# Attention with soft mixture of experts on one core: whole columns of the last three w2 matrices, full output rows, and a tile of its own for the first pair's q and k

## The chip, the cores and the metric

The kernel runs on one core of a Trainium2 chip. The metric is device time in microseconds; the time before is 157.08 us, the median of 7 runs (156.41 to 157.62). TensorE, VectorE, ScalarE, GpSimd and SyncE are called PE, DVE, ACT, POOL and SP, as in the profile.

## The reference

There are two stages. The first is attention with 4 batches, 8 heads, 768 positions and a head dimension of 64; each head has either the full causal mask or a mask of sink positions and a window. Its output is laid out as x, 3072 tokens by 512. The second is a soft mixture of 8 experts with 4 slots each:

```python
logits = x @ phi                                   # 3072 x 32
d = softmax of logits over the tokens
slot_input = (d.T @ x).reshape(8, 4, 512)
for e in range(8):
    h = np.maximum(slot_input[e] @ w1[e], 0.0)     # w1[e]: 512 x 1024
    slot_out[e] = h @ w2[e]                        # w2[e]: 1024 x 512
c = softmax of logits over the slots
return c @ slot_out.reshape(32, 512)               # 3072 x 512, float32
```

All inputs and the output are float32 in memory.

## The kernel before

**Order of work.** The order of the instructions on each engine is the order in which the code is written; tiles give the waits. All loads go through POOL's DMA queue and are cast from float32 to bf16 on the way: q, k, v, phi, and w1 and w2 of the eight experts. A tile pool with two buffers (`raw`, used in `load_qk`, L106) holds the raw q and k, so the load of a third piece waits until the transposes of the first have read it. `load_qk([0])`, `load_qk([1])`, `load_v(0)` and the first w1 are issued before the loop; at the start of step 0 of the loop come `load_qk([2])` and `load_v(1)`.

**Attention.** The loop over `n` goes through 16 pairs of heads. A step computes the scores of pair `n` in six chunks (L167), their exponentials on ACT (L172), masks them on DVE (L184), multiplies the pair before with its values (L193) and transposes q and k of the pair after (L141). `w_load` spreads the loads of the weights over the loop; w1 is complete and w2 of experts 0 to 4 is issued there.

**The last three w2.** The w2 of experts 5, 6 and 7 have no place until attention lets go of memory: expert 5 takes the place of the masks, 6 and 7 those of the two exponential tiles. They are loaded in halves of 256 columns by `w_half` (L399): first the left halves of all three, then the right halves. The memory layout is `(fi fo) d -> fi fo d`, so that one partition reads 8 consecutive rows of w2; a half takes 256 columns of each of them.

**The experts.** After the slot inputs, the products with w1 (L481) and the transposes of the hidden layer (`turn`, L497), the products with w2 collect in two PSUM tiles, `sp[0]` for the left and `sp[1]` for the right 256 columns. They use 32 output partitions at a time, in four groups of partitions; `second` (L513) multiplies one expert. As expert 5, 6 and 7 have four rows only, their products may go to any of the four groups: what follows sums the groups. 24 small products (L530) give the sums by which an output row is divided (`rrow`).

**Output.** The output is 24 blocks of rows: partition `p` holds rows 24p to 24p+23. Each block is one product with `slot_out` (L541), scaled on DVE if its number is even (L545) and on ACT if odd (L543), and stored by a DMA together with its neighbours. The order before is this. The left columns of experts 5 to 7 are multiplied, `slot_out`'s left half is copied (L556), and the left halves of blocks 0 to 11 are made and stored from POOL's queue. Then come the right columns of experts 5 to 7, the copy of the right half (L560), blocks 12 to 23 in full, stored from SP's queue (L568), and at last the right halves of blocks 0 to 11, also from SP's queue (L554).

Of the kernel before, what the change touches and what calls it, by code (L numbers as in the profile page):

```python
# [10 lines left out]
F32 = mybir.dt.float32  # L11
BF16 = mybir.dt.bfloat16
I32 = mybir.dt.int32
ALU = mybir.AluOpType
ACT = mybir.ActivationFunctionType
# [23 lines left out]
def kernel(  # L39
# [13 lines left out]
    nc = tc.nc  # L53
    P = 128
    B, H, S, D = q.shape
    n_sink, window = int(n_sink), int(window)
    ES = moe_phi.shape[1]
    NE, DM, F = moe_w1.shape
    SPE = ES // NE
    scale = 1.0 / (D ** 0.5)  # L60
# [4 lines left out]
    raw = ent(tc.tile_pool(name="raw", bufs=2))  # L65
# [9 lines left out]
    def single(shape, dt, name, tag=None):  # L75
        return singles.tile(shape, dt, name=name, tag=tag or name)

    w1s = [single([P, 4, F], BF16, f"w1_{e}") for e in range(NE)]
    w2s = [single([P, 8, DM], BF16, f"w2_{e}") for e in range(NE - 3)] + [None] * 3
# [7 lines left out]
    rrow = single([P, 24], F32, "rrow")  # L87
# [7 lines left out]
    slot_out = single([P, DM], BF16, "slot_out")  # L95
# [9 lines left out]

    def load_qk(pairs, order="qk"):  # L106
        b, h, c = pairs[0] // 4, 2 * (pairs[0] % 4), 2 * len(pairs)
        t = raw.tile([P, 2, 2, S], BF16, tag="raw", name="raw")
        for which in order:
            src, d, z = (q, qraw, 0) if which == "q" else (k, kraw, 1)  # L110
            nc.gpsimd.dma_start(t[:, z, :len(pairs)],  # L111
                                src[b, h:h + c].rearrange("(y h) (p s) d -> (h p) y (s d)", h=2, s=12))
            for x, n in enumerate(pairs):
                d[n] = t[:, z, x]

    def load_v(m):
        b, h = m // 2, 4 * (m % 2)
        nc.gpsimd.dma_start(vbs[m % 3].rearrange("p h j d -> p (h j) d")[:, :, :D],  # L118
                            v[b, h:h + 4].rearrange("h (j p) d -> p (h j) d", p=P))
# [5 lines left out]
    w2v = [moe_w2[e].rearrange("(fi fo) d -> fi fo d", fo=8) for e in range(NE)]  # L125
    wi = [1]

    def w_load(upto):
        while wi[0] < min(upto, 2 * NE - 3):
            e = wi[0] % NE  # L130
            dst, src = ((w1s, w1v), (w2s, w2v))[wi[0] // NE]
            nc.gpsimd.dma_start(dst[e], src[e])
            wi[0] += 1
# [89 lines left out]
    def logits_exp(b):  # L223
        nc.scalar.activation(expT[:, b], lgs[b][:96], ACT.Exp, accum_out=colpart[:, b:b + 1])  # L224
# [29 lines left out]
                   allow_small_or_imprecise_dtypes=True)  # L254
    load_qk([1])
    load_v(0)
    nc.gpsimd.dma_start(w1s[0], w1v[0])

    V = nc.vector
# [3 lines left out]
    def keep_busy(t, count):  # L263
        for _ in range(count):
            nc.tensor.matmul(t, zero[:, :P], zero, start=True, stop=True)  # L265

    idle = pvp.tile([P, 512], F32, tag="pv", name="idle")
# [23 lines left out]
    def head_mask(h):  # L291
        V.tensor_scalar(msk[:, h], grade, thr[:, h:h + 1], None, op0=ALU.is_ge)
# [26 lines left out]

    for n in range(NP):  # L320
        if n == 0:
            load_qk([2])
            load_v(1)
        elif n == 1:
            load_qk([3])
        elif n == 2 or (n % 2 == 1 and n < 12):
            m = 2 if n == 2 else (n + 3) // 2
            load_qk([2 * m, 2 * m + 1])
            load_v(m)
        w_load(1 + 5 * (n + 1) // 8)  # L330
        if n == 0:
            nc.gpsimd.dma_start(phi, moe_phi.rearrange("(do di) s -> di do s", di=P))
        b, r = n // 4 - 1, n % 4
        last = n - 1

        scores(n, 0)
        if n >= 1:
            for i in range(3):
                pvmm(last, i)
        if b >= 0 and r == 2:  # L340
            logits_mm(b, (0, 1, 2, 3))

        scores(n, 1)
        if b >= 0 and r == 2:
            logits_exp(b)
        if n >= 1:
            norm(last, 0)
        if 0 < n < NP - 1:
            tq = transposes(n + 1, "q")
            evac(n + 1, "q", tq)  # L350
        mask(n, 0)
        if b >= 0 and r == 3:
            exp_tokens(b)

        scores(n, 2)
        if n >= 1:
            pvmm(last, 3)
        if n >= 2:
            x_transpose(n - 2)
        mask(n, 1)  # L360

        scores(n, 3)
        if 0 < n < NP - 1:
            tk = transposes(n + 1, "k")
        mask(n, 2)

        scores(n, 4)
        if 0 < n < NP - 1:
            evac(n + 1, "k", tk)
        if n >= 1:  # L370
            pvmm(last, 4)
        if n:
            vfar(n)

        scores(n, 5)
        if n == 0:
            vfar(0)
        if n >= 1:
            pvmm(last, 5)
            norm(last, 1)  # L380
        if b >= 0 and r == 3:
            dispatch_mm(b)
            slot_sum(b)
        if n == 0:
            evac(1, "q", transposes(1, "q"))
            evac(1, "k", transposes(1, "k"))
        if n < 3:
            far_mask(n + 1)
            for h in (2 * n + 2, 2 * n + 3):
                head_mask(h)  # L390
        elif n == 3:
            setup_late()


    w_load(2 * NE)
    left, right, full = slice(0, 256), slice(256, 512), slice(0, 512)

    def w_half(e, cs):
        nc.gpsimd.dma_start(w2s[e][:, :, cs], w2v[e][:, :, cs])  # L399

    w2s[5] = single([P, 8, DM], BF16, "w2_5", tag="msk")
    w_half(5, left)
    w2s[6] = ptp.tile([P, 8, DM], BF16, tag="pT", name="w2_6")
    w_half(6, left)


    def bank(t, shape=(P, 512), dt=F32):
        pool, tag = ((scp, "sc"), (trp, "tr"), (pvp, "pv"))[t]
        return pool.tile(list(shape), dt, tag=tag, name="bank")
# [27 lines left out]
    copies(1, 0)  # L437
    logits_mm(bl, (0, 1, 2))
    w2s[7] = ptp.tile([P, 8, DM], BF16, tag="pT", name="w2_7")
    w_half(7, left)  # L440
    for e in (5, 6, 7):
        w_half(e, right)
    x_transpose(last, 0, 3)
    x_transpose(last, 3, 6)
    copies(2, 0)
    idle = bank(2)
# [11 lines left out]
    idle = bank(2)  # L458
# [10 lines left out]
    cs = bank(1, (P, 1))  # L469
# [5 lines left out]
    for e4 in range(2):  # L475
        t = xp.tile([P, 2, 512], BF16, tag="xb", name="hs")
        for c in range(2):
            hp = bank(0 if e4 == 0 else 2)
            for do in range(4):
                for g in range(4):  # L480
                    nc.tensor.matmul(hp[32 * g:32 * g + 32], siT[:, do],  # L481
                                     w1s[4 * e4 + g][:, do, c * 512:(c + 1) * 512],
                                     start=(do == 0), stop=(do == 3))
# [6 lines left out]
    hT = {}  # L490
# [14 lines left out]
    sp = [t[:, 0, :256] for t in spt]  # L505
    idle = spt[1][:, 1]

    def second(e, xs=(0, 1), spread=False):
        e4, g = e // 4, e % 4
        for fo in range(8):  # L510
            c = fo % 4 if spread else g
            for x in xs:
                nc.tensor.matmul(sp[x][32 * c:32 * c + 32, :], hT[e4][:, fo, 32 * g:32 * g + 32],  # L513
                                 w2s[e][:, fo, 256 * x:256 * x + 256],
                                 start=(e4 == 0 and fo == 0), stop=(e == 7 and fo >= 4))

    turn(0)
    for fo in range(8):
# [2 lines left out]
                nc.tensor.matmul(sp[x][32 * g:32 * g + 32, :], hT[0][:, fo, 32 * g:32 * g + 32],  # L521
                                 w2s[g][:, fo, 256 * x:256 * x + 256], start=(fo == 0), stop=False)
    turn(1)
    second(4, spread=True)
    rp = bank(2, (P, 24))
    er = []
    for r in range(24):
        e = expR.rearrange("c (p r) -> c r p", r=24)[:, r]
        er.append(e)
        nc.tensor.matmul(rp[:, r:r + 1], e[:ES], ones[:ES], start=True, stop=True)  # L530
    V.reciprocal(rrow, rp)
    for e in (5, 6, 7):
        second(e, (0,), spread=True)


    NL = 12
    ov = out.rearrange("(p r) d -> p r d", r=24)

    def product(r, o, cs, t):
        op = bank(t, (P, cs.stop - cs.start))  # L540
        nc.tensor.matmul(op, er[r], slot_out[:, cs], start=True, stop=True)  # L541
        if r % 2:
            nc.scalar.activation(o, op, ACT.Copy, scale=rrow[:, r:r + 1])  # L543
        else:
            V.tensor_scalar(o, op, rrow[:, r:r + 1], None, op0=ALU.mult)  # L545

    def half_rows(cs, t0, groups, banks, eng):
        ots = [single([P, n, 256], F32, f"oh{t0 + x}", tag=f"w1_{t0 + x}") for x, n in enumerate((8, NL - 8))]
        r = 0
        for rows in groups:  # L550
            for _ in range(rows):
                product(r, ots[r // 8][:, r % 8], cs, banks[r % len(banks)])
                r += 1
            eng.dma_start(ov[:, r - rows:r, cs], ots[(r - 1) // 8][:, (r - rows) % 8:(r - 1) % 8 + 1])  # L554

    V.tensor_copy(slot_out[:, left], sp[0])  # L556
    half_rows(left, 0, (2, 2, 4, 4), (1, 2), nc.gpsimd)
    for e in (5, 6, 7):
        second(e, (1,), spread=True)
    V.tensor_copy(slot_out[:, right], sp[1])  # L560
    r = NL
    for t, groups in enumerate(((1, 1, 2), (4,), (4,))):
        ot, base = single([P, 4, DM], F32, f"ot{t}", tag=f"w1_{4 + t}"), r
        for rows in groups:
            for _ in range(rows):
                product(r, ot[:, r - base], full, (1, 2)[r % 2])
                r += 1
            nc.sync.dma_start(ov[:, r - rows:r, :], ot[:, r - rows - base:r - base])  # L568
    half_rows(right, 2, (4, 4, 4), (1, 2), nc.sync)


# [33 lines left out]
```

The softmax here doesn't subtract the row's maximum and nothing guards it: scores larger than these inputs give would overflow.

## Time and profile before

| What | Value |
|---|---|
| Median of 7 runs | 157.08 us |
| Profiled execution, its own time | 157.49 us |
| Span of the profiled execution | 155.7 us |
| PE, DVE, ACT, POOL busy | 119.8, 107.2, 110.4, 41.2 us |
| Mean granted TensorE clock | 0.891 |
| HBM read, written | 52.49 MB, 6.29 MB |
| Loads of a whole w1 or w2 (13, 1024 KB in bf16) | median 17.5 us from issue to landing |
| Loads of half a w2 (6, 512 KB in bf16) | median 16.3 us from issue to landing |

The span is from the first to the last instruction; the time of an execution is 1.8 us longer than the span of the profiled one. The time to landing of a DMA includes its wait in the queue behind the DMAs issued before it. The row that tells of the DMA engines gives the mean busy share of the 16 of them; a share over 1 in a narrow window means that packets of one engine overlap.

### The profile page before, as it was taken

The page shows a single profiled execution, that of the slowest core. Times are in us where ns is not written, and L with a number is a line of the kernel's source. Part 1 is how long each engine was busy: PE and PEld are TensorE (multiplying, and loading weights), DVE is VectorE, ACT ScalarE, POOL GpSimd, SP SyncE. Part 2 cuts the span into 40 slices and gives each one's busy share as a digit, 9 for nine tenths or more (in the row PEclk, how much of TensorE's full clock was granted, in tenths as well). Part 3 has the DMA queues.
Part 4 walks back from the last instruction along what each step waited for, and adds up shares of the span by engine and source line. Part 5 has one row for each costly group of instructions (what it writes and reads, how often), then busy time and mean ns, then how long its engine had stood idle before and what let it go on. Part 6 is the DMA issues. An engine that isn't in the chain of part 4 may idle for free. (4 is left out here: it accounts for less than half of the span.)

```text
span 155.7 us, 5049 instructions
## 1 busy us (share of the span) xinstructions
PE 119.8 (77%) x2237; PEld 75.7 (49%) x2239; DVE 107.2 (69%) x247; ACT 110.4 (71%) x148; POOL 41.2 (26%) x57
## 2 busy tenths in 40 slices
PE   6766597888597979979779989797887988949500
PEld 2324365555355656556456556564552476514300
DVE  2896279999958769879688897786854331719700
ACT  3286479989789898999998999999643311608700
POOL 7673033720350080070048200000453000510000
PEclk9965559999959999999999999999999999557965
DMA  3999999999999999999999999999999999997995
GB/s 44 163 170 203 177 211 207 198 183 184 222 213 201 191 211 200 187 221 193 188 223 192 188 226 208 213 223 208 225 210 192 198 198 197 184 344 288 415 355 183
DMA packets 40535, 32.85 MB, mean 211 GB/s; under 512 B 26050, under 2 KB 37826, under 8 KB 38594
## 3 DMA queue, kind: packets, MB, share of 16 engines
q0 software_dynamic: 38208, 27.82, 115.6%
q1 hardware_dynamic: 2306, 4.72, 8.1%
q8 instruction: 17, 0.28, 0.6%
q14 instruction: 4, 0.03, 0.1%
HBM read 52.49 MB, written 6.29 MB: 378 GB/s over the span
## 5 line engine op out<-in xcount | busy, mean ns | idle before, releaser
L172 ACT ACTIVATE pT<-sc 128x1024 bf16<-128x1024 f32 (+1 forms) x96 | 83.8, 922 | 10.6 <-PE sc L167 9.8
L167 PE MATMUL sc<-Tq,Tk 64*128 64x256 bf16 (+3 forms) x320 | 37.2, 297 | 13.6 <-ACT Tk L151 10.2
L193 PEld LDWEIGHTS <-pT 128*128 128x128 bf16 x672 | 25.2, 100 | 12.5 <-issue 8.3
L184 DVE TENSOR_TENSOR pT<-pT,msk 128x1024 bf16<-128x1024 bf16 (+1 forms) x48 | 29.4, 639 | 0.2 <-ACT pT L172 0.2
L193 PE MATMUL pv<-vb,pT 128*128 128x65 bf16 x352 | 27.9, 198 | 0.3 <-DVE xb L202 0.3
L193 PE MATMUL pv<-vf,pT 128*128 128x65 bf16 x320 | 25.5, 198 | 0.0
L167 PEld LDWEIGHTS <-Tk 64*128 64x128 bf16 x320 | 11.3, 95 | 22.9 <-ACT Tk L151 13.2
L141 PEld LDWEIGHTS <-raw 64*64 64x64 bf16 x768 | 16.1, 115 | 11.0 <-issue 8.5
L111 POOL DMA_DIRECT2D raw<-in_q_dram x10 | 6.4, 641 | 50.9 <-PE tpk L141 49.7
L148 DVE COPY Tq<-tpq 128x768 bf16<-128x768 bf16 x16 | 15.3, 956 | 6.1 <-PE tpq L141 5.9
L202 DVE TENSOR_TENSOR xb<-pv,rs 128x384 bf16<-128x384 f32 x32 | 17.8, 557 | 1.1
L151 ACT COPY Tk<-tpk 128x768 bf16<-128x768 bf16 x16 | 12.8, 803 | 4.8 <-PE tpk L141 4.8
L201 DVE RECIPROCAL rs<-pv 128x6 f32<-128x6 f32 x32 | 6.2, 194 | 12.5 <-PE pv L193 12.3
L118 POOL DMA_DIRECT2D vb<-in_v_dram x8 | 11.6, 1452 | 1.1 <-issue 0.9
L399 POOL DMA_DIRECT2D w<-in_moe_w_dram x6 | 5.3, 882 | 24.4 <-PE sc L167 22.2
L141 PE MATMUL tpk<-ident,raw 64*64 64x64 bf16 x384 | 9.6, 200 | 2.3 <-DVE Tq L148 2.3
L141 PE MATMUL tpq<-ident,raw 64*64 64x64 bf16 x384 | 9.9, 203 | 1.7 <-DMA raw<-in_q_dram 1.7
L541 PE MATMUL bank<-slot_out,expR 128*128 128x256 bf16 (+1 forms) x35 | 9.4, 385 | 1.9 <-DVE slot_out L556 0.5
L210 PE MATMUL tpx<-ident,xb 128*128 128x128 bf16 x96 | 8.1, 218 | 2.0 <-ACT expT L224 1.1
L211 DVE COPY xT<-tpx 128x768 bf16<-128x768 bf16 (+1 forms) x17 | 9.0, 529 | 0.8 <-PE tpx L210 0.8
L543 ACT ACTIVATE oh<-bank,rrow 128x256 f32<-128x256 f32 x12 | 5.3, 474 | 4.3 <-PE bank L541 4.1
L541 PEld LDWEIGHTS <-expR 128*128 128x128 bf16 x36 | 5.3, 153 | 6.1 <-issue 5.2
(86 smaller groups left out, 116.4 us busy)
## 6 DMA issues: line engine op xcount, KB each, us to landing
w<-in_moe_w_dram POOLq DMA_DIRECT2D x13, 1024.0 KB, 17.5
vb<-in_v_dram POOLq DMA_DIRECT2D x8, 384.0 KB, 12.0
w<-in_moe_w_dram POOLq DMA_DIRECT2D x6, 512.0 KB, 16.3
raw<-in_q_dram POOLq DMA_DIRECT2D x6, 384.0 KB, 9.0
raw<-in_k_dram POOLq DMA_DIRECT2D x6, 384.0 KB, 10.2
out_dram<-ot SPq DMA_DIRECT2D x2, 1024.0 KB, 4.6
out_dram<-oh SPq DMA_DIRECT2D x3, 512.0 KB, 6.3
out_dram<-oh POOLq DMA_DIRECT2D x2, 512.0 KB, 5.4
```

Source lines behind the costliest of these rows:

```text
L118: nc.gpsimd.dma_start(vbs[m % 3].rearrange("p h j d -> p (h j) d")[:, :, :D], v[b, h:h + 4].rearrange("h (j p) d -> p (h j) d", p=P))
L141: nc.tensor.transpose(tp[po, s, :], src[po, 64 * s:64 * s + 64], ident[po, po])
L148: nc.vector.tensor_copy(o, i)
L151: nc.scalar.copy(o, i)
L167: nc.tensor.matmul(sc[:, hh, at:at + 128 * cnt], kT[n][po:po + 64, j * 128:(j + 1) * 128], qT[n][po:po + 64, i0 * 128:(i0 + cnt) * 128], s ...
L172: nc.scalar.activation(pT[n][:, :, o:o + ln], sc[:, :, :ln], ACT.Exp, scale=scale)
L184: nc.vector.tensor_mul(x, x, m)
L193: nc.tensor.matmul(pv[n][:, i % 3, hh, :], pT[n][:, hh, o:o + 128], vv[:, hh, j, :D + 1], start=(j == 0), stop=(j == i))
L202: nc.vector.tensor_mul(xb[b][:, 3 * half:3 * half + 3, h * D:(h + 2) * D].rearrange("p i (h d) -> p i h d", h=2), pv[n][:, :, :, :64], rs. ...
L210: nc.tensor.transpose(tp[:, i * 128:(i + 1) * 128], xb[b][:, i, hp * 128:(hp + 1) * 128], ident)
L211: nc.vector.tensor_copy(xT[:, hp, i0 * 128:i1 * 128], tp[:, i0 * 128:i1 * 128])
L541: nc.tensor.matmul(op, er[r], slot_out[:, cs], start=True, stop=True)
```

## The change

Three things are changed.

1. The first pair's q and k get a tile of their own (`raw0`), so that the two buffers of `raw` serve from pair 1 on. `load_qk([2])` moves from the start of the loop, where it stood behind the load of the first w1, to a place ahead of that load.
2. The w2 of experts 5 and 6 are loaded whole, in one DMA each; that of expert 7 in two pieces, of which the first holds six of the eight `fo` (768 KB in bf16) and the second the last two (256 KB), both with all columns.
3. The products with w2 are done for both halves of the columns at once, expert by expert, with two warming products (`keep_busy`) ahead of expert 7. Behind the second piece of expert 7 stand four products, one in each group of partitions. Then `slot_out` is copied, the left half on DVE and the right half on ACT, and 24 full output blocks are made; blocks 0 and 1 are made in halves, of which DVE scales the left and ACT the right. All stores go through SP's queue, in groups of 1, 1, 2 and five times 4 blocks. The early left halves are gone.

```diff
     def load_qk(pairs, order="qk"):
-        t = raw.tile([P, 2, 2, S], BF16, tag="raw", name="raw")
+        if pairs == [0]:
+            t = single([P, 2, 1, S], BF16, "raw0")
+        else:
+            t = raw.tile([P, 2, 2, S], BF16, tag="raw", name="raw")
...
     load_v(0)
+    load_qk([2])
     nc.gpsimd.dma_start(w1s[0], w1v[0])
...
         if n == 0:
-            load_qk([2])
             load_v(1)
...
-    w_half(5, left)
+    nc.gpsimd.dma_start(w2s[5], w2v[5])
-    w_half(6, left)
+    nc.gpsimd.dma_start(w2s[6], w2v[6])
...
-    w_half(7, left)
-    for e in (5, 6, 7):
-        w_half(e, right)
+    for fos in (slice(0, 6), slice(6, 8)):
+        nc.gpsimd.dma_start(w2s[7][:, fos], w2v[7][:, fos])
...
-    second(4, spread=True)
+    second(4, range(8), (0, 0, 1, 1, 2, 2, 3, 3))
+    second(5, range(8), (0, 0, 1, 1, 2, 2, 3, 3))
...
     V.reciprocal(rrow, rp)
-    for e in (5, 6, 7):
-        second(e, (0,), spread=True)
+    second(6, range(8), (0, 0, 1, 1, 2, 2, 3, 3))
+    keep_busy(idle, 2)
+    second(7, range(6), (0, 0, 1, 1, 2, 2, 3, 3))
+    second(7, range(6, 8), (0, 1, 2, 3))
...
-    V.tensor_copy(slot_out[:, left], sp[0])
-    half_rows(left, 0, (2, 2, 4, 4), (1, 2), nc.gpsimd)
-    for e in (5, 6, 7):
-        second(e, (1,), spread=True)
-    V.tensor_copy(slot_out[:, right], sp[1])
+    V.tensor_copy(slot_out[:, :256], sp[0])
+    nc.scalar.copy(slot_out[:, 256:], sp[1])
...
-    for t, groups in enumerate(((1, 1, 2), (4,), (4,))):
+    for t, groups in enumerate(((1, 1, 2), (4,), (4,), (4,), (4,), (4,))):
+        ot, base = single([P, 4, DM], F32, f"ot{t}", tag=f"w1_{t}"), r
...
+                if r < 2:
+                    for x in range(2):
+                        cs = slice(256 * x, 256 * x + 256)
+                        op = bank((1, 2)[x], (P, 256))
+                        nc.tensor.matmul(op, er[r], slot_out[:, cs], start=True, stop=True)
+                        if x:
+                            nc.scalar.activation(o[:, cs], op, ACT.Copy, scale=scale)
+                        else:
+                            V.tensor_scalar(o[:, cs], op, scale, None, op0=ALU.mult)
+                else:
+                    op = bank((1, 2, 0)[r % 3])
+                    nc.tensor.matmul(op, er[r], slot_out, start=True, stop=True)
...
             nc.sync.dma_start(ov[:, r - rows:r, :], ot[:, r - rows - base:r - base])
-    half_rows(right, 2, (4, 4, 4), (1, 2), nc.sync)
```

More of the change, by code (lines that the diff above doesn't have):

```diff
@@ L395 @@
     w_load(2 * NE)
-    left, right, full = slice(0, 256), slice(256, 512), slice(0, 512)
-    def w_half(e, cs):
-        nc.gpsimd.dma_start(w2s[e][:, :, cs], w2v[e][:, :, cs])
     w2s[5] = single([P, 8, DM], BF16, "w2_5", tag="msk")
-    w_half(5, left)
+    nc.gpsimd.dma_start(w2s[5], w2v[5])
     w2s[6] = ptp.tile([P, 8, DM], BF16, tag="pT", name="w2_6")
-    w_half(6, left)
+    nc.gpsimd.dma_start(w2s[6], w2v[6])
     def bank(t, shape=(P, 512), dt=F32):
@@ L506, with second @@
     idle = spt[1][:, 1]
-    def second(e, xs=(0, 1), spread=False):
+    ends = {(0, 0): 6, (1, 1): 6, (0, 2): 7, (1, 3): 7, (1, 0): 4, (0, 1): 5, (1, 2): 2, (0, 3): 3}
+    def second(e, fos, groups):
         e4, g = e // 4, e % 4
[L510 to L515, printed above, removed]
+        for z, (fo, x) in enumerate((fo, x) for fo in fos for x in range(2)):
+            c = groups[z % len(groups)]
+            nc.tensor.matmul(sp[x][32 * c:32 * c + 32, :], hT[e4][:, fo, 32 * g:32 * g + 32],
+                             w2s[e][:, fo, 256 * x:256 * x + 256], start=False,
+                             stop=(e == 7 and ends[x, c] == fo))
     turn(0)
@@ L531 @@
     V.reciprocal(rrow, rp)
-    for e in (5, 6, 7):
-        second(e, (0,), spread=True)
-    NL = 12
-    ov = out.rearrange("(p r) d -> p r d", r=24)
[L539 to L549, printed above, removed]
+    second(6, range(8), (0, 0, 1, 1, 2, 2, 3, 3))
@@ L550, in half_rows @@
+    keep_busy(idle, 2)
[3 more added lines that the diff above has]
+    nc.scalar.copy(slot_out[:, 256:], sp[1])
+    ov = out.rearrange("(p r) d -> p r d", r=24)
+    r = 0
+    for t, groups in enumerate(((1, 1, 2), (4,), (4,), (4,), (4,), (4,))):
+        ot, base = single([P, 4, DM], F32, f"ot{t}", tag=f"w1_{t}"), r
         for rows in groups:
             for _ in range(rows):
-                product(r, ots[r // 8][:, r % 8], cs, banks[r % len(banks)])
@@ L553, in half_rows @@
-                r += 1
-            eng.dma_start(ov[:, r - rows:r, cs], ots[(r - 1) // 8][:, (r - rows) % 8:(r - 1) % 8 + 1])
-    V.tensor_copy(slot_out[:, left], sp[0])
-    half_rows(left, 0, (2, 2, 4, 4), (1, 2), nc.gpsimd)
-    for e in (5, 6, 7):
-        second(e, (1,), spread=True)
-    V.tensor_copy(slot_out[:, right], sp[1])
-    r = NL
-    for t, groups in enumerate(((1, 1, 2), (4,), (4,))):
[L563 to L566, printed above, removed]
+                o = ot[:, r - base]
@@ new lines @@
+                scale = rrow[:, r:r + 1]
+                if r < 2:
[10 more added lines that the diff above has]
+                    nc.tensor.matmul(op, er[r], slot_out, start=True, stop=True)
+                    if r % 2:
+                        nc.scalar.activation(o, op, ACT.Copy, scale=scale)
+                    else:
+                        V.tensor_scalar(o, op, scale, None, op0=ALU.mult)
```

## The prediction

> **What bounds the kernel now.** I read the DMA rows by windows first, then the chain that ended last, then the tail of the timeline engine by engine, then single DMAs from issue to landing. The windows (columns: stretch, its length, TensorE clock, DMA share, GB/s):
>
> ```profile
> 12.00:16.00 4.00, 0.50 1.01 207
> ...
> 92.00:96.00 4.00, 1.00 1.07 223
> ...
> 128.00:132.00 4.00, 0.99 1.45 197
> 132.00:136.00 4.00, 0.50 1.23 187
> 136.00:140.00 4.00, 0.50 1.01 334
> 140.00:144.00 4.00, 0.73 0.74 286
> 144.00:148.00 4.00, 1.00 1.02 416
> 148.00:152.00 4.00, 0.62 1.01 354
> ```
>
> From 4 us on the 16 DMA engines are full in every window until 140 us. Loads run near 200 GB/s (as written, in bf16; twice that is read), stores near 400. The one hole is in 140 to 144 (share 0.74): the stores' first data are not ready yet. The chain of waits (start, length, what) says the same:
>
> ```profile
> 116.64 0.47 PE bank L265 x2
> 117.11 20.95 DMA w<-in_moe_w_dram
> 138.05 0.04 issue
> 138.09 0.64 PE bank L513 x7
> 138.76 0.44 DVE slot_out L560
> ...
> 139.24 1.01 PE bank L541 x2
> ```
>
> The last right half of w2 (issued at 117.11, landed at L = 138.05) ends the loads; all compute is waiting for it. Behind it come a short chain and the stores. The kernel is thus a stream of loads, a gap, and a stream of stores, and what counts is how much of the stores lies behind L. The stores:
>
> ```profile
> 134.06 3.03 POOL L554 DMA_DIRECT2D out_dram<-oh  x4 [16.07 <-DVE oh L545]
> 140.64 4.22 SPq L568 DMA_DIRECT2D out_dram<-ot  x5
> 145.41 2.05 SPq L554 DMA_DIRECT2D out_dram<-oh  x2
> ```
>
> The four early stores (12 left half rows, 1.57 MB) are issued at 134.06 to 136.3 and take 4.7 to 5.7 us to land, so until 142.0. They fill the DMA engines while the last loads and the chain behind L are under way (334 GB/s in 136 to 140). The other 4.72 MB are issued from 140.64 on.
>
> **The change, part by part. Early load of pair 2: 0 on the time.** It removes this wait of PE (and 1.2 us of POOL's for the buffer):
>
> ```profile
> 18.35 0.85 PE L141 MATMUL tpq<-ident,raw 64*64 64x64 bf16 x24 [1.67 <-DMA raw<-in_q_dram]
> ```
>
> Both DMAs of pair 2 pass one DMA on POOL's queue, w1 of expert 0 (1024 KB), which lands about 2 us later and is first read at 121 us. `load_v(1)` and phi stay behind both. Compute may run up to 1.7 us earlier, or nothing if pair 3, which is loaded no earlier, stops it again. It doesn't matter: the DMA queue has work throughout and its sum is unchanged, and PE then waits for w2 at the end in any case. Its bounds are 0 and, if compute set the end, -1.7; a loss needs the queue to run dry, and it holds 4 us or more of work. I take 0.
>
> **Whole w2 instead of halves: L moves from 138.05 to 136.6.** Asked one at a time, the last whole loads (L132) were issued at 83.4, 83.9, 84.4, 85.8 and 87.8 and took 18.2, 22.5, 26.9, 30.3 and 33.2 us: they landed at 101.6, 106.4, 111.3, 116.1 and 121.0, 4.85 us apart. The six halves landed at 123.7, 127.2, 129.5, 132.2, 135.4 and 138.05. That is 17.0 us for 3 MB, with steps of 2.3 to 3.5. The regular step is about 2.65 (15.9 in all); 1.1 us are irregular. Both long steps have an instruction fetch on the DMA engines just before them; the queue table gives 17 of these with a 0.6% share, 0.6% x 16 x 155.7 / 17 = 0.9 us of one engine each, and a load has landed only when the slowest engine is done. Three whole loads are 3 x 4.85 = 14.55; the last piece of 256 KB is in packets of 2 KB, between the 512 B of the halves (5.3 us per MB) and the 8 KB of whole loads (4.85), so at most 0.1 more. That gives L = 121.0 + 14.65 = 135.65 without the irregular part, and 136.75 with all of it. PE's program up to there has the same length within some ten instructions, so the fetches come at about the same places: I take 136.6.
>
> Here a rule stands against the change. The Trainium skill, "DMA: Bandwidth & Descriptors", section Specifications, puts the smallest transfer for the full rate at 512 B. A half row of w2 in bf16 is just 512 B, and by the rule whole rows gain nothing: L would be 138.0 and the sum 1.4 us worse. The rows (2.65 us against 4.85 / 2 = 2.43 for 512 KB) decide for a gain of 0.2 us per half; a part of it could be the irregularity, which is why the upper end of my range keeps it out.
>
> **No early stores: does L gain by that too?** The first is issued at 134.06, behind all loads in the same queue, so an engine can turn to it only when its own share of the loads is done. I take 0; the bound on the other side is the rival below.
>
> **The chain behind L: -0.7.** Before, from L to the first store's issue: 140.64 - 138.05 = 2.6 us, made of eight products in two rounds on the four groups (0.64), the copy (0.42 and waits), a product of 512 columns (0.62 until DVE starts) and its scaling (0.74). After: one round of four (-0.2), both copies side by side (DVE 0.42; ACT's nearest row, 128x256 scaled in L543, 0.47: +0.05), a product of 256 columns (-0.2) and two scalings of 256 side by side (0.47 instead of 0.74: -0.3). 2.6 - 0.65 = 1.9 us.
>
> **PE's work ahead of L: 0.** The products of expert 5 move ahead of the 24 small ones, with 16 more products (0.5 us from 16 in 0.82). They and expert 6 end near 132.4 and two warming products follow; expert 7's first piece lands near 135. The wait of some 3 us covers them.
>
> **The stores: +3.5 us.** Before, from the first issue at 140.64, eight full rows (2.1 MB) are landed at 147.2 (issue 143.3 + 3.9), 6.6 us later; the next four at 144.5 + 5.3 = 149.8, so 2.6 us per MB; the three half groups 1.5 us each for 0.5 MB, until 154.35; the end of the span follows 1.35 later. Sum 6.6 + 2.6 + 4.5 + 1.35 = 15.05, and 155.7 - 140.64 = 15.06. After: eight rows 6.6, four groups of four rows 4 x 2.63 = 10.5, and 1.35: 18.5 us. So +3.45: the half rows' 1.57 MB behind L get cheaper by 0.6, and 1.57 MB more at 2.63 per MB come behind L, 3.95. DVE and ACT don't bound this: 4 rows take them 2 x 0.74 = 1.5 us, a store of them 2.63. Nor does PE: at half clock a 512-column product takes 0.43, four take 1.7. SP's issue of a full-row store is 0.33 to 0.42.
>
> **Sum.** 136.6 + 1.9 + 18.5 = 157.0 of span against 155.7: +1.3. The profiled execution's own time is 157.49, 0.4 above the median of 157.08, which its neighbours also reach (156.41 to 157.62), so I put the difference on the median: 158.4.
>
> **The rivals.**
>
> - The irregular part of the loads disappears (the fetches fall on an engine that is ahead) and the first rows follow faster than before. L = 135.65, span 156.05 or a little less: 157.4, the same. For it: whole loads before 121 land 4.85 apart although fetches go on there as well.
> - The kernel gets faster, because the early stores had held back the last loads. Place: the window 132 to 136, where the rate falls to 187 GB/s as stores start. At 197 GB/s the halves would have ended by 135.4 on average instead of 138.05; with 1.25 for whole rows L = 134.1, span 134.1 + 20.4 = 154.5, time 155.9. It decides as soon as L is below 135.3, where the span equals 155.7. Against it: the step before the last half (132.2 to 135.4) was as long with no store under way.
> - The stores don't keep 400 GB/s for so long: the same page's limit per core for HBM is 358 GB/s. Then 6.29 MB take 17.6 instead of 16.5 (2.63 per MB): about 159.5, or 160 if the first megabyte also starts late. The rows, two groups at 2.6 us, speak against it, and 354 GB/s in 148 to 152, with half rows in it, for it.
>
> **How the numbers follow.** A measurement of this kernel can tell about 0.5% from no change (156.3 to 157.9). Likeliest, 0.57: exposed stores with most of the irregular part, 158.4 (own range 157.8 to 158.9). Same, 0.25: 157.4 (156.9 to 157.9). Faster by held-back loads, 0.08: 155.9. Slow stores, 0.10: 159.5 and more. Slower: 0.54 of the first and the last case, 0.64. Same: 0.03 + 0.23 + 0.01 = 0.27. Faster: 0.09. The range leaves out most of the last two cases: 156.9 to 159.3.
>
> **What would show it.** Right: the last w2 piece lands at 135.7 to 136.8; the first store is issued 1.9 us later; DMA share drops well under 0.7 for some 3 us behind L and before it as engines finish one by one; from then on full-row groups land 2.6 us apart, the last 17 us after the first issue; PE's 1.67 us wait at 18 us is gone and L132's landings are not moved by more than 0.3 us. Wrong: L132's last landing moved (the early load did something to the stream), L under 135.3, or groups landing under 2.45 us apart.

## The result, and the profile after

The changed kernel takes 158.42 us (median of 27 runs, 157.56 to 160.44) against 157.25 us for the kernel before (64 runs): a ratio of 1.0092, 95% interval 1.0073 to 1.0111. It is some 1.4 us slower; the ratio leaves out, for both kernels, the executions more than 1.5% above the fastest, and so is a little larger than that of the medians. The forecast was 158.4 us, and a span of 157.0 us; the profiled execution has a span of 157.1 us and a time of its own of 158.89 us.

The windows of the changed kernel, in the same columns as before (stretch, length, TensorE clock, DMA share, GB/s):

```profile
124.00:128.00 4.00, 1.00 1.01 210
128.00:132.00 4.00, 1.00 1.03 212
132.00:136.00 4.00, 0.60 0.44 85
136.00:140.00 4.00, 0.50 0.10 37
140.00:144.00 4.00, 0.62 0.89 357
144.00:148.00 4.00, 1.00 1.04 426
148.00:152.00 4.00, 0.73 1.02 424
152.00:156.00 4.00, 0.50 0.80 330
```

Two things have changed. Loads of whole rows move 210 to 212 GB/s until 132 us, where the halves moved 197. And from 132 to 140 us the DMA engines run empty: their busy share is 0.44 and then 0.10, where it was over 1 before. The trace shows when each of the 16 engines reports its share of the last load: the first at 132.31, the last at 136.65, on average at 134.1. So the average engine stands idle for 2.5 us ahead of the last landing, and only the rest of the hole is the chain behind it. The early stores had filled both.

Between 132 and 144 us the kernel before moved (187 + 334 + 286) x 4 us = 3.23 MB and the changed one (85 + 37 + 357) x 4 us = 1.92 MB. The missing 1.31 MB take 3.3 us at 400 GB/s; that is what the early stores had been worth. Some 2 us of it come back, by an estimate from the windows. Up to 132 us the changed kernel has moved 26.21 MB and the one before 25.88, which is 0.8 us. Behind 144 us it has more left to move (4.72 MB against 3.74), but without half rows it moves that at some 400 GB/s against 361, which is 1 us for 3.74 MB.

The chain of waits that ended last (start, length, what):

```profile
112.96 0.52 POOL w L439
113.48 23.17 DMA w<-in_moe_w_dram
136.65 0.04 issue
136.69 0.45 PE bank L511 x4
137.15 0.42 DVE slot_out L537
137.57 0.04 issue
137.61 1.01 PE bank L551 x4
138.62 4.28 PE bank L558 x10
```

The last piece of w2 lands at L = 136.65 us instead of 138.05. Four products, the copies and the products of the first blocks follow; the first store is issued at 138.73:

```profile
138.73 9.34 SPq L564 DMA_DIRECT2D out_dram<-ot  x8
```

Before, 15.1 us passed from the first store behind the last load to the end of the span; now it is 157.1 - 138.73 = 18.4 us. Counted from L, it was 17.7 us to the end and is now 20.5. So the last load lands 1.4 us earlier, what follows takes 2.8 us longer, and the difference is the 1.4 us of the result.

### The profile page after: what moved, and what is told of

Its sections match the earlier page's. It is cut to its first block, busy times and chain, and to the rows that moved or that the text cites. A ratio compares the mean times of both kernels' runs of the same rounds, so it can differ in the third digit from the quotient of the medians.

```text
span 157.1 us, 5010 instructions
## 1 busy us (share of the span) xinstructions
PE 119.3 (76%) x2229; PEld 75.0 (48%) x2231; DVE 106.5 (68%) x241; ACT 109.6 (70%) x144; POOL 34.8 (22%) x51
## 5 line engine op out<-in xcount | busy, mean ns | idle before, releaser
L170 PE MATMUL sc<-Tq,Tk 64*128 64x256 bf16 (+3 forms) x320 | 36.7, 294 | 14.1 <-ACT Tk L154 10.5
L196 PE MATMUL pv<-vb,pT 128*128 128x65 bf16 x352 | 27.4, 196 | 0.3 <-DVE xb L205 0.3
L558 PE MATMUL bank<-slot_out,expR 128*128 128x512 bf16 x22 | 8.0, 500 | 0.6 <-ACT ot L560 0.6
L562 DVE TENSOR_SCALAR ot<-bank,rrow 128x512 f32<-128x512 f32 x11 | 8.0, 749 | 0.6 <-PE bank L558 0.2
L560 ACT ACTIVATE ot<-bank,rrow 128x512 f32<-128x512 f32 x11 | 7.3, 688 | 1.3 <-PE bank L558 1.0
L213 PEld LDWEIGHTS <-xb 128*128 128x128 bf16 x96 | 6.3, 100 | 2.8 <-issue 2.7
```

Of the source, the lines that this page charges most:

```text
L170: nc.tensor.matmul(sc[:, hh, at:at + 128 * cnt], kT[n][po:po + 64, j * 128:(j + 1) * 128], qT[n][po:po + 64, i0 * 128:(i0 + cnt) * 128], s ...
L196: nc.tensor.matmul(pv[n][:, i % 3, hh, :], pT[n][:, hh, o:o + 128], vv[:, hh, j, :D + 1], start=(j == 0), stop=(j == i))
L213: nc.tensor.transpose(tp[:, i * 128:(i + 1) * 128], xb[b][:, i, hp * 128:(hp + 1) * 128], ident)
L558: nc.tensor.matmul(op, er[r], slot_out, start=True, stop=True)
L560: nc.scalar.activation(o, op, ACT.Copy, scale=scale)
```

## The experiments

Times scatter by some 0.6 us from one execution to the next (standard deviation), so what a profile shows is also given as the time from L to the end of its span. That leaves out when the loads happened to end.

**The first part alone, and all but the first part.** The first kernel adds the early load to the kernel before; the second takes it out of the changed kernel.

```diff
-        t = raw.tile([P, 2, 2, S], BF16, tag="raw", name="raw")
+        if pairs == [0]:
+            t = single([P, 2, 1, S], BF16, "raw0")
+        else:
+            t = raw.tile([P, 2, 2, S], BF16, tag="raw", name="raw")
...
     load_v(0)
+    load_qk([2])
...
-            load_qk([2])
             load_v(1)
```

> The kernel before with the first part of the change alone: raw0 for the first pair and the load of pair 2 ahead of the first w1. My theory: 0 (within 0.3 us of before); PE's wait of 1.67 us at 18 us is gone, and the last w2 half still lands at 138.0, give or take 0.5. Rival: the early load shifts the stream of loads (in the profile of the changed kernel the last whole load ahead of experts 5 to 7 landed at 122.0 instead of 121.0); then the last half lands near 139.0 here and the time is 1 us worse than before.

> The changed kernel without the first part: pair 0 in the shared buffers, the load of pair 2 back behind the first w1. My theory: the same as the changed kernel, 158.4 (within 0.3). Rival, by which the early load delays the loads by 1.0 us: 157.4, with the last piece of w2 landing near 135.7.

Measured: alone on the kernel before 1.0024 (0.9989 to 1.0059), 157.62 against 157.34 us, last half landed at 137.7. The changed kernel without it: 159.28 us, 1.0110 (1.0074 to 1.0145), not told apart from the changed kernel's 1.0092, with the last piece at 137.2. Taking the early load out did not bring the landing back to 135.7, so it is not what moved it. In the changed kernel PE's wait at 18 us is gone, as the transposes of pair 2 show (timeline: start, length, instruction). But a wait of the same kind stands at a later pair, where the kernel before has none:

```profile
16.70 0.85 PE L144 MATMUL tpq<-ident,raw 64*64 64x64 bf16 x24
...
30.50 0.85 PE L144 MATMUL tpq<-ident,raw 64*64 64x64 bf16 x24 [1.09 <-DMA raw<-in_q_dram]
```

In the kernel with the early load alone this wait is 2.67 us. So the early load moves the wait to a later pair, much as the prediction had held possible. The end of attention has no common direction either: the last exponential ends at 113.3 us with the early load alone and at 111.4 before, at 109.9 in the changed kernel and at 110.4 without the early load. Of all this no gain reaches the end.

**Half loads in the changed kernel.** Everything else stays, so this parts the rows' length from the early stores.

```diff
...
-    nc.gpsimd.dma_start(w2s[5], w2v[5])
+    w_half(5, left)
...
-    nc.gpsimd.dma_start(w2s[6], w2v[6])
+    w_half(6, left)
...
-    for fos in (slice(0, 6), slice(6, 8)):
-        nc.gpsimd.dma_start(w2s[7][:, fos], w2v[7][:, fos])
+    w_half(7, left)
+    for e in (5, 6, 7):
+        w_half(e, right)
```

> The changed kernel with the w2 of experts 5 to 7 loaded as before, in six halves of 256 columns, left ones first; no early stores. My theory (short rows make the loads slower, the early stores did not hold them back): the last half lands at 138.0, give or take 0.5, as before; behind it come the 16 products of expert 7 instead of four, so the first store is issued some 3.0 us later and the time is 2.0 to 2.6 us above the changed kernel, about 160.7. Rival of the rule of 512 B (row length doesn't matter): the last half lands at 136.6, the time is 0.6 to 1.0 above the changed kernel. Rival of the held-back loads: without early stores the halves are all landed by 135.4, and the time is near that of the changed kernel or below it.

Measured: 160.69 us, 1.0201 (1.0151 to 1.0250). From its chain of waits:

```profile
117.41 20.44 DMA w<-in_moe_w_dram
137.85 0.04 issue
137.90 1.31 PE bank L517 x12
139.20 0.42 DVE slot_out L543
```

L is 137.85 with no early store under way, so the early stores had not held the loads back. From there to the end it takes 21.1 us, against 17.7 in the kernel before, whose L is nearly the same. So leaving the early stores out costs 3.4 us by the profiles, of which 0.6 lie in the first eight blocks, whose chain is longer here; by the times it is 2.0% or 3.2 us. Loading whole instead of in halves, with the shorter chain that goes with it, gives back 1.7 us (1.0201 against 1.0092). The two together are the change's 1.4.

The last whole load landed at 121.54 here, and the six halves took 16.3 us; in the changed kernel the same 3 MB took 14.65. Taken on the engine that finishes first, which leaves out what delays single engines, the 3 MB take 15.92 to 15.93 us in all three kernels that load them in halves (here and with the early load alone as well as before, with and without early stores). They take 15.48 with expert 5 whole, 15.04 with experts 5 and 6 whole, and 14.64 to 14.65 in the five profiles of kernels that load as the changed one does: 0.4 us for each expert. The rule of 512 B that the prediction cites, by which the rows' length would not matter, does not hold here: rows of 512 B cost 1.3 us per 3 MB more than the longer ones (8 KB, and 6 and 2 KB for expert 7). The number of packets changes with the rows, and the runs do not part the two. The first store is issued at 140.79, 2.9 us after L.

**The long chain in the changed kernel.**

```diff
-    nc.scalar.copy(slot_out[:, 256:], sp[1])
+    V.tensor_copy(slot_out[:, 256:], sp[1])
...
-                if r < 2:
+                if r < 0:
```

> The changed kernel with the longer chain behind the last piece: both halves of slot_out copied on DVE, blocks 0 and 1 made as full products. My theory: 0.4 for the second copy, 0.2 for the product of 512 columns and 0.3 for its scaling on one engine, so the first store is issued some 0.8 us later and the time is 0.7 to 0.9 above the changed kernel, since nothing covers the chain: the DMA engines are idle in it. Rival (the chain is covered, or the stores catch up because later blocks are ready sooner than stored): under 0.3.

Measured: 159.20 us, 1.0108 (1.0069 to 1.0146). The interval holds the changed kernel's 1.0092 and the 0.8 us of the theory as well, so the times do not decide. The profile does: from L to the end it takes 20.7 us instead of 20.5, and the theory fell. The first store is issued at 139.28, 2.7 us after L = 136.59, so the chain is 0.6 us longer, nearly as expected. But the fourth store, the first of four full blocks, has these rows in the view of its line, for this DMA alone:

```profile
L564 SPq DMA_DIRECT2D out_dram<-ot x1: 332/332/332, 142.0 to 142.0; - x1
DMA to landing us min/median/max: 3.9/3.9/3.9
```

and these in the changed kernel:

```profile
L564 SPq DMA_DIRECT2D out_dram<-ot x1: 332/332/332, 141.9 to 141.9; - x1
DMA to landing us min/median/max: 3.9/3.9/3.9
```

They are issued 5.4 and 5.3 us after L. The store waits for block 7, and PE makes the blocks at 0.43 us each while its clock is at 0.5; four half products for two blocks (1.0 us) are no faster than two full ones. The short chain brings the first 0.5 MB out earlier, and the stores then wait for the next blocks. (The clock rose to 1.0 at 141.0 here and at 143.0 in the changed kernel; that is about when block 7 is made, so it can have hidden little of the longer chain.)

**More warming products in the changed kernel.**

```diff
+    keep_busy(idle, 5)
     second(6, range(8), (0, 0, 1, 1, 2, 2, 3, 3))
-    keep_busy(idle, 2)
+    keep_busy(idle, 10)
```

> The changed kernel with more warming products: 5 ahead of expert 6 and 10 instead of 2 ahead of expert 7, so that PE has no gap over 1 us until the last piece lands. In the changed kernel PE's clock is 0.5 from about 132.9 us until 143, and the first full group of four blocks is issued 5.2 us after the last piece, when its products at 0.43 us each are done. My theory: at full clock the chain is 0.3 us shorter and the first full group is ready 1 us earlier, so the hole in the DMA windows 142 to 144 closes: 0.5 to 0.9 us below the changed kernel, about 157.7. Rival: the first stores are bound by DMA latency and the scalings on DVE and ACT (0.7 us a block each), not by the clock: under 0.2. If the warming products overrun the landing, the time is worse by up to 1 us.

Measured: 158.19 us, 1.0060 (1.0023 to 1.0097). The interval overlaps with the changed kernel's, so the gain of some 0.5 us is likely, not shown. The mechanism shows in the windows of this kernel (stretch, length, PE busy, clock, DMA share, GB/s), where the clock stays at 1.00 until 144 and no hole is left between 140 and 148:

```profile
132.00:136.00 4.00, 4.00 (x40) 1.00 0.44 87
136.00:140.00 4.00, 3.16 (x29) 1.00 0.02 4
140.00:144.00 4.00, 3.26 (x13) 1.00 1.00 393
144.00:148.00 4.00, 1.77 (x6) 0.96 1.03 424
```

From L = 137.53 to the end it takes 19.65 us, 0.8 less than in the changed kernel, and all of it lies in the first eight blocks: the fourth store is issued 4.1 us after L instead of 5.3 and has landed 8.4 us after it instead of 9.2. In this execution L was 0.9 us later, so that the span is the same, 157.2.

**Two groups of stores left out.** Blocks 16 to 23 are neither made nor stored, so a third of the output is missing.

```diff
-    for t, groups in enumerate(((1, 1, 2), (4,), (4,), (4,), (4,), (4,))):
+    for t, groups in enumerate(((1, 1, 2), (4,), (4,), (4,))):
```

> The changed kernel without the last two groups of four output blocks: blocks 16 to 23 are neither made nor stored (2.1 MB of 6.29 left out). My theory: the stores lie open behind the last piece of w2, at 2.5 us per MB as the last groups of the changed kernel land (2.49 apart), so the time falls by 5.0 us to about 153.4. Rival: the end is set by making the blocks (PE, DVE, ACT at 0.35 us a block) and not by the stores; then 8 blocks less are worth 2.8 us, 155.6.

Measured: 153.65 us, 0.9793 (0.9729 to 0.9856) and 4.8 us below the changed kernel (1.0092 - 0.9793 = 0.0299 of 157.4 is 4.7, give or take 1 by the interval). From L to the end it takes 15.0 us, 5.4 less. So the stores are what lies open behind L, at 2.3 us per MB by the times and 2.6 by the profiles; the blocks' making, 2.8 us, would have been too little.

**Expert 5 whole, the rest as before.** This was measured twice.

```diff
-    w_half(5, left)
+    nc.gpsimd.dma_start(w2s[5], w2v[5])
...
-    for e in (5, 6, 7):
+    for e in (6, 7):
         w_half(e, right)
```

> The kernel before with w2 of expert 5 loaded whole, and nothing else. My theory: two short-row halves become one whole load, 5.3 us become 4.85, so 0.3 to 0.5 us below before, about 156.9. Rival (the slowest engine, not the length of rows, sets the landing): no difference.

> The kernel before with w2 of expert 5 loaded whole, once more, as its first comparison (0.9968, 0.9934 to 1.0002) did not part it from the kernel before. My theory: 0.3 to 0.5 us faster than before, 0.9975. Rival: the same as before, 1.000.

Measured: 156.61 us, 0.9968 (0.9934 to 1.0002), and 157.10 us, 0.9983 (0.9949 to 1.0017). Both are on the side that was expected, by 0.3 to 0.5 us, and neither parts it from the kernel before. They fit the 0.4 us per expert that the landings show.

**Expert 5 whole and 16 early blocks.** The loads are those of the kernel just above; beyond them:

```diff
...
-    NL = 12
+    NL = 16
...
-    half_rows(left, 0, (2, 2, 4, 4), (1, 2), nc.gpsimd)
+    half_rows(left, 0, (2, 2, 4, 4, 4), (1, 2), nc.gpsimd)
...
-    for t, groups in enumerate(((1, 1, 2), (4,), (4,))):
+    for t, groups in enumerate(((1, 1, 2), (4,))):
...
-    half_rows(right, 2, (4, 4, 4), (1, 2), nc.sync)
+    half_rows(right, 2, (4, 4, 4, 4), (1, 2), nc.sync)
```

> The kernel before with two changes: w2 of expert 5 is loaded whole (6 and 7 still in halves), and 16 instead of 12 blocks have their left halves made and stored early. My theory: 0.4 us from the whole load, and 0.5 MB more of early stores fills the hole of about 1 us in which the DMA engines of the kernel before wait for the first full rows, less 0.2 us for more half rows at the end: 0.8 to 1.3 us below before, about 156.2. Rival: the additional early products stand ahead of the right columns in PE's order and delay the chain behind the last half as much as they fill; then no change, 157.3.

Measured: 157.94 us, 1.0046 (1.0018 to 1.0075), slower than before. The hole it was to fill is not there in the kernel with expert 5 whole: with 12 early blocks the windows of that kernel (stretch, length, PE busy, clock, DMA share, GB/s) read

```profile
136.00:140.00 4.00, 2.66 (x31) 0.87 0.93 304
140.00:144.00 4.00, 3.45 (x14) 1.00 1.02 381
```

where the kernel before had 286 GB/s and 0.74 from 140 to 144. The second profile of that kernel agrees (384 GB/s and 1.03). The early stores start later there (134.8 against 134.1 us) and the first full row is issued earlier (139.9 and 140.0 against 140.6), so that they meet. Whole rows are not the only way to that: with the early load alone, and halves throughout, the window has no hole either (364 GB/s and 1.01). What is left of the addition is its cost, more half rows; this is argued, not tested. From L to the end it takes 18.4 us, with 12 early blocks 17.9. The ratios are 1.0 to 1.2 us apart, give or take 0.7; whether more than this 0.5 is behind that is open. The rival does not show: the first full row is issued 2.2 us behind L with 16 early blocks, and 2.2 and 2.6 with 12.

**Experts 5 and 6 whole, expert 7 in halves, 8 early blocks.**

```diff
...
-    w_half(5, left)
+    nc.gpsimd.dma_start(w2s[5], w2v[5])
...
-    w_half(6, left)
+    nc.gpsimd.dma_start(w2s[6], w2v[6])
...
-    for e in (5, 6, 7):
-        w_half(e, right)
+    w_half(7, right)
...
-    NL = 12
+    NL = 8
```

The products with experts 5 and 6 are then done for both halves at once, and the groups of blocks follow NL: 2, 2, 4 early, 16 full, and 4, 4 at the end.

> The kernel before with the w2 of experts 5 and 6 loaded whole, only expert 7 in halves, and 8 instead of 12 left half blocks made early, behind expert 7's left half. It lies between the changed kernel (no halves, no early stores) and the kernel with expert 5 whole. My theory: the last half lands at about 136.6 to 137.0; the left half is there 2.65 us earlier, so the early stores begin about when the loads end and cover the chain behind the last half, but not the time before it in which engines run empty one after another. 18.7 us of stores and end behind that: a span of 155.3 to 155.7 and 156.6 to 157.2 of time, as good as with expert 5 whole. Rival (any store moved behind the loads costs in full): 16 of 24 blocks' time is uncovered as in the changed kernel, 157.8 or more.

Measured: 159.23 us, 1.0094 (1.0050 to 1.0139), as slow as the changed kernel. The rival was right. From its chain, its timeline and its windows (stretch, length, PE busy, clock, DMA share, GB/s):

```profile
115.09 19.27 DMA w<-in_moe_w_dram
134.35 0.04 issue
134.40 0.64 PE bank L512 x8
...
135.06 0.43 DVE slot_out L556
...
135.54 1.96 PE bank L541 x8
137.49 0.58 PE bank L512 x5
```

```profile
137.02 2.19 POOL L554 DMA_DIRECT2D out_dram<-oh  x3 [20.16 <-DVE oh L545]
```

```profile
136.00:140.00 4.00, 3.47 (x19) 0.50 0.42 135
```

The left half lands at 134.35, and 2.7 us pass until its first store at 137.02, by which time the last half has landed (137.0). The early stores then start too late to fill the time in which the engines run empty (share 0.42 from 136 to 140), and their products stand ahead of the last ones on PE. PE's clock was at 0.5 from 131.4 to 141.7 us; whether this placement of the stores would pay at full clock was not tried.

## Why the prediction was right, step by step

- **The early load, 0:** not contradicted. Neither kernel that parts it off is told apart from its neighbour, to within some 0.6 us. The claim that L132's landings would not move by more than 0.3 us failed: the last whole load landed 1.0 us later. The prediction had named just that as a sign of being wrong, with the early load as its cause; without the early load that landing was at 122.55, later still, so the sign came up for another reason (next point).
- **L at 136.6:** 136.65, but by luck, as two errors cancel. The three experts took exactly the regular 14.65 us, so the "irregular part" of up to 1.1 us, of which I had kept most, did not occur in them. The last whole load ahead of them landed 1.0 us later instead: issued at 87.57, 34.4 us to landing, so 122.0 against 121.0. The first engine to finish that load was even 0.4 us earlier than before. The gap between the first and the last grew from 3.2 to 4.3 us between the loads that landed at 96.5 and 102.5, and an instruction fetch had begun at 98.7. So the irregular part is real and of the right size (a fetch is 0.9 to 1.0 us of one engine), but it may fall anywhere in the stream: in five profiles of kernels with these loads it added 0 (three times), 0.3 and 1.1 us to the last three experts. I had tied it to the place where it fell in one execution.
- **No gain of L from leaving out the early stores:** right; half loads without early stores landed at 137.85, and on the first engine the last 3 MB took as long as before to 0.01 us.
- **The chain, -0.7:** the first store came 2.1 us after L, not 1.9, and 2.7 with the long chain. But the end moved by only 0.1 to 0.2. This step failed as a saving. I had the first eight blocks land 6.6 us after the first store whenever that was issued. The changed kernel lands them 145.8 - 138.73 = 7.1 us after it (the store at 141.9 took 3.9). Counted from L it is 9.2 us before, 9.2 in the changed kernel and 9.3 with the long chain: the saving is nil. What sets it is PE's products at half clock, as the 8.4 us with more warming products show. I had ruled PE out as a bound (four products in 1.7 us against 2.63 for storing them), which holds only once stores are queued ahead.
- **The stores, 18.5 us with the end:** 18.4. My 2.63 was one interval between two groups of four (147.2 to 149.8), not two. The 0.5 us lost on the first eight blocks came back from the later groups, which land 2.49 us apart instead of 2.63: 4 x 0.14 = 0.6.
- **The rivals:** the stores did keep their rate (424 GB/s from 148 to 152), so the limit of 358 GB/s that the prediction cites did not bind here. The page cited there, the Trainium skill's "DMA: Bandwidth & Descriptors", gives this figure under Bandwidth as each core's part when both cores of an HBM domain stream; here one core ran. The kernel did not become faster by freed loads. The case "same" came near: without the irregular part the sum would have given 157.4, and some executions ended at 157.6.

So the likeliest case was right in its mechanism: stores that had been covered by loads and by the chain were put behind both. That the total fits so closely is luck, since the terms for the irregular part, the chain and the rate of the groups were each off by 0.5 us or more, in both directions.

## What to carry to other kernels

When a kernel is a stream of loads, a short chain and a stream of stores, a store moved from under the last loads to behind them can cost its full transfer time. Here shorter loads gave back half of that and a shorter chain nothing. So count the bytes that the DMA engines move in the windows around the last landing, before and after. A shorter chain to the first result is worth only what the whole first large transfer gains; look for what that one waits for (here products at half clock). When 16 engines share the loads, the last landing is that of the slowest: the first was free 4 us earlier here, and stores that are ready by then can fill that time. Before costing a gap between two landings as regular or irregular, look at how far apart the first and the last of the 16 engines report, and leave chance events as a spread on the result and not as a part of one step.

## What the runs showed of the hardware

- The first and the last of the 16 DMA engines to finish the same load were 2.0 to 5.3 us apart at the load of expert 4's w2, in the profiles of the kernels run here. Steps of 0.3 to 1.2 us in this gap came after an instruction fetch (0.9 to 1.0 us of one engine) had started: at 98.6 in the changed kernel without the early load, at 115.8 with half loads, at 125.1 with expert 5 whole. Most fetches left no step (in the changed kernel those at 104.8, 113.7, 123.3 and 131.5). That these fell on engines that were not last would fit, but the trace does not name a packet's engine. Nor was it tested that fetches make much of the 0.6 us of scatter between executions.
- Stores in groups of four full blocks (1 MB, 8 KB packets) landed 2.49 us apart in the changed kernel, 421 GB/s. In the kernels that store full rows alone the interval was 2.48 to 2.54 us; in those with half rows behind the full ones it was up to 2.67. Why is open.
- PE's clock stood at 0.5 from 132.8 to 143.0 us in the changed kernel, with a wait of 1.6 us and two warming products ahead of its fall and a wait of 2.5 us behind it. With fifteen warming products PE had no gap over 0.9 us from 119 us until its last product, and the clock stayed at 1.0 from 123.8 to 147.7 us.
